# Score stacks moved by 64 bytes and score products widened to 64 rows, in an attention block gated by a bilinear GLU

## The chip, the cores and the metric

The kernel runs on one core of one Trainium2 chip. Its time is the device time of one execution in microseconds. Three runs of the kernel before the change gave 2594.28, 2596.97 and 2593.94 us; the median is 2594.28 us.

## What is computed

```
x: [1, 2048, 576]      D = 576, H = 32 heads of Dh = 18, F = 4608
xn   = layernorm(x)
q,k,v = heads of xn @ wqkv
s    = softmax(q k^T * Dh^-0.5) v   for each head;  s = concat(heads) @ wo
g    = silu(((xn @ w_gate) * (xn @ w_up)) @ w_down)
out  = x + s * g
```

Everything is float32. The kernel keeps float32 accuracy with TensorE's faster float32r format by splitting each operand into a high part (rounded to float32r) and a low part (the rest), and by summing the products high x high, low x high and high x low.

## The kernel before

**Prologue** (up to about 193 us). x is normalised, transposed with TensorE into columns, and split into high and low parts. `xc` (or `xcx`, for the first two chunks of 512 tokens) holds one chunk of columns: nine planes of 128 x 512. `qk_block` (L488) makes one 128-column block of q and k for one chunk with 14 whole-array matmuls (L493): weights from `wgu`, `wq1`, `wq2` or `ninth`, columns as the moving operand. Its high and low parts go to the DRAM tensor `sqk`. `v_block` (L550, matmuls at L556) makes v. There are nine column blocks and four chunks; blocks 4 and 5 take their weights from `wq2`, block 8 from `wq1`.

**Score stacks.** After the pool `early` is closed, three tiles of 128 partitions x 2048 float32 are made in the pool `stk`: `turning`, `whole0`, `whole1`. A stack holds, in partitions 0 to 53 and again in 64 to 117, three copies of 18 rows (one head's q or k, high or low). One matmul over these 54 rows (R = 54) gives the three split products at once. `load_stack` (L317) fills them from `sqk` with three DMAs each, issued on SP's queue. Before that, GpSimd sets all three tiles to 1.0 (L638, L641).

**Main stage** (about 193 to 2512 us). TensorE's array is used as two halves of 64 rows that run side by side, each with its own chain of matmuls. Four kinds of products are mixed in an order that a planner writes out by hand at build time, with fixed costs (0.231 us for a 512-column product, 0.132 us for a down product):

- `a_item` (L701, matmul L709): a 128 x 512 tile of scores, 54 rows, mostly on half 0. VectorE reduces it to a row maximum (L711). There are 2048 of them.
- `b_item` (L754, matmul L761): the same scores transposed, mostly on half 1, with 56 rows: rows 54 and 55 of the half carry the negative maximum (high and low part, written by `max_rows`, L733) against ones in the other operand. ScalarE takes the exponential (L763). There are 2048 of them.
- `gu_op` (L810, matmul L813): gate and up products of 64 rows x 128 by 64 x 512, 7776 of them; and `down_op` (L871, matmul L874): 64 rows x 128 by 64 x 288, 6912 of them.
- `pv_group` (L767, matmul L772): probabilities times v, on the whole array, in 7 us blocks.

Scores go to two banks `pa` and two banks `pb`, the rest to four banks `pg`; each product waits by semaphore until its bank has been emptied. **The end** (from 2512 us) multiplies by `wo` and writes out.

Where the operands lie, as byte offsets in a partition, and that offset modulo 256, from the program's memory map:

| tile | offset | mod 256 | role |
|---|---|---|---|
| xc | 59,552 and 77,984 | 160 | moving operand of L493 and L813; weights of L556 |
| wgu | 27,296 and 36,512 | 160 | weights of L493 and L813 |
| hs | 113,312 and 121,504 | 160 | weights of L874 |
| wd | 50,336 (half of its columns begin 1152 bytes further) | 160 and 32 | moving operand of L874 |
| wq1 | 185,760 | 160 | weights of L493 |
| wq2, xn | 220,128 and 209,888 | 224 | weights of L493; weights of the transposes |
| turning, whole0, whole1 | 204,768, 212,960, 221,152 | 224 | both operands of L709 and L761 |

Every slice of these tiles that a 512-column product takes begins a multiple of 256 bytes further on. `early` and `stk` are pools on the right side of the memory: they end at its upper end, one after the other in time.

Of the kernel before, what the change touches and what calls it, by code (L numbers as in the profile page):

```python
# [20 lines left out]
FT = mybir.dt.float32  # L21
# [20 lines left out]
def kernel(  # L42
# [10 lines left out]
    nc = tc.nc  # L53
# [46 lines left out]
    ep = early.enter_context(tc.tile_pool(name="early", bufs=1, side="right"))  # L100
# [18 lines left out]
    def w_split(raw, n, pool=None):  # L119

        if pool:
            w = pool.tile([128, n, 9, 128], FR, name=f"wq{n}")
        else:
            w = wpool.tile([128, 2, 9, 128], FR, name="wgu", bufs=2)
        ninth = pp.tile([128, 2, 128], FR, name="ninth", bufs=4)

        def piece(i, d, n, src, high=True, rest=True):
            if high:
                nc.scalar.activation(w[:, i, d:d + n, :], raw[:, i, src:src + n, :], AF.Copy)
            if not rest:  # L130
                return
            low = w[:, i, 4 + d:4 + d + n, :] if d < 8 else ninth[:, i:i + 1, :]
            op = nc.gpsimd.tensor_tensor(low, raw[:, i, src:src + n, :],
                                         w[:, i, d:d + n, :].bitcast(FT), op=OP.subtract)
            if behind:
                after(op, behind.pop(), "DVE's fast mode and Pool share a port")

        return (w, ninth), [(piece, a) for i in range(n) for a in ((i, 0, 4, 0), (i, 8, 1, 4))]
# [170 lines left out]
    R = 3 * DH  # L309
# [36 lines left out]
    def load_x(c, ts=range(4)):  # L346
        if ts[0] == 0:
            xin[c] = ep.tile([128, 4, D], FT, name="xin", bufs=2)
        for t in ts:
            nc.sync.dma_start(xin[c][:, t, :], x2[c * 512 + t * 128:c * 512 + t * 128 + 128, :])  # L350
# [28 lines left out]
    def norm(c, ts=range(4)):  # L379
        for t in ts:  # L380
            norm_stats(c, t)
        for t in ts:
            norm_apply(c, t)
# [3 lines left out]
    def to_columns(c):  # L387

        xn = xns.pop(c)
        if c < 2:  # L390
            xc = pp.tile([128, 9, 512], FR, name="xcx", bufs=2)
        else:
            xc = xcp.tile([128, 9, 512], FR, name="xc")
        xcs[c] = xc
        for k in range(5):
            if k < 4:
                p = bank("g", 3)
            else:
                p = bank("a" if nqk[0] % 2 else "b", 2)
                nqk[0] += 1  # L400
            for t in range(4):
                nc.tensor.transpose(p[:, t * 128:(t + 1) * 128],  # L402
                                    xn[:, t, k * 128:(k + 1) * 128], ident)
            if k < 4:
                nc.scalar.activation(xc[:, k, :], p, AF.Copy)
                nc.vector.tensor_tensor(xc[:, 4 + k, :], p, xc[:, k, :].bitcast(FT),
                                        op=OP.subtract)
            else:
                nc.scalar.activation(xc[:, 8, :], p, AF.Copy)
                nc.vector.tensor_tensor(xc[64:128, 8, :], p[64:128, :],  # L410
                                        xc[64:128, 8, :].bitcast(FT), op=OP.subtract)
# [76 lines left out]
    def qk_block(b, c):  # L488
        w, ninth = (t[:, b % 2] for t in wq[b // 2])
        p = bank("a" if nqk[0] % 2 else "b", 2)  # L490
        nqk[0] += 1
        for n, (a, e) in enumerate(QK_PAIRS):
            nc.tensor.matmul(p, w[:, a, :] if a < 9 else ninth, xcs[c][:, e, :], start=n == 0,  # L493
                             stop=n == len(QK_PAIRS) - 1)
        hl = pp.tile([128, 2, 512], FR, name="hl", bufs=3)
        nc.scalar.activation(hl[:, 0, :], p, AF.Copy)
        nc.vector.tensor_tensor(hl[:, 1, :], p, hl[:, 0, :].bitcast(FT), op=OP.subtract)
        g0 = blocks[b]
        for kind in range(2):
            lo, hi = max(g0, kind * D), min(g0 + 128, (kind + 1) * D)  # L500
            if lo < hi:
                dst = sqk[kind, :, lo - kind * D:hi - kind * D, c * 512:(c + 1) * 512]
                nc.sync.dma_start(dst.rearrange("h r s -> r h s"), hl[lo - g0:hi - g0].bitcast(FT))
# [40 lines left out]
    def v_split(h):  # L544
        cs = slice(h * HALF, (h + 1) * HALF)
        for k, d, lo in V_PARTS:
            nc.scalar.activation(vbox["w"][:, d, cs], vbox["raw"][:, k, :], AF.Copy)
        v_low(h)
# [18 lines left out]
    def w_now(i):  # L567
        wq[i], todo = w_split(raws[i], 1 if i == 4 else 2, ep if i == 2 else pp if i == 4 else None)
        for f, a in todo:
            f(*a)  # L570

    def w_fetch(i):
        raws[i] = w_load([(wqkv, b) for b in blocks[2 * i:2 * i + 2]])

    def x_store(c, ks):
        for k in ks:
            src = xcs[c][:, k, :].bitcast(FT)
            if k < 8:
                nc.sync.dma_start(sx[c, 2 * (k % 4):2 * (k % 4) + 2, :, k // 4, :].rearrange("b p s -> (b p) s"), src)
                if k % 4 == 0:  # L580
                    nc.sync.dma_start(sx[c, 9, :, k // 4, :], src[0:64])
            else:
                for part in range(2):
                    nc.sync.dma_start(sx[c, 8, :, part, :], src[64 * part:64 * part + 64])
# [22 lines left out]
    for c in range(NCH):  # L607
        if c + 2 < NCH:
            load_x(c + 2)
        for b in range(3):  # L610
            qk_block(b, c)
            if c == 0 and b == 0:
                w_now(2)
        if c + 1 < NCH:
            to_columns(c + 1)
        for b in range(3, 6):
            qk_block(b, c)
            if c == 1 and b == 3:
                v_split(c)
            if b < 5 and c + 2 < NCH:  # L620
                norm(c + 2, (0, 1) if b == 3 else (2, 3))
            if c in (1, 2):
                x_store(c, range(3 * (b - 3), 3 * (b - 2)))
            if c == 0 and b == 3:
                v_fetch(1)
            if c == NCH - 1 and b == 3:
                w_now(3)
        if c == 1:
            w_fetch(3)
            for t in range(4):  # L630
                v_block(t)
            w_fetch(4)
        if c == 2:
            w_now(4)
    early.close()
    stk = ctx.enter_context(tc.tile_pool(name="stk", bufs=1, side="right", reuse_waits="tile"))
    turning = stk.tile([128, S], FR, name="turning")
    nc.gpsimd.memset(turning.bitcast(FT), 1.0)  # L638
    whole = [stk.tile([128, S], FR, name=f"whole{i}") for i in range(2)]
    for w in whole:  # L640
        nc.gpsimd.memset(w.bitcast(FT), 1.0)  # L641
    vmore = ExitStack()
    more_rows(vmore.enter_context(tc.tile_pool(name="vmore", bufs=1, side="right")), 2)
    g_load(0)
# [46 lines left out]
    with ExitStack() as mid:  # L691
# [3 lines left out]
        def load_v(g):  # L695
            vt[g] = mp.tile([128, NT, 2 * (DH + 1)], FT, name="vt", bufs=2)
            nc.sync.dma_start(vt[g].rearrange("p t (h d) -> p t h d", h=2), sv[:, 2 * g:2 * g + 2, :].rearrange("(t p) h d -> p t h d", p=128))

        mx = {}

        def a_item(h, i, r=0, tag="a"):  # L701

            t, c = divmod(i, 4)
            if i == 0:
                mx[h] = mp.tile([128, NT, 4], FT, name="mx", bufs=1)
            q, k = stacks_of(h, r)
            p = bank(tag, 2)
            rows = slice(64 * r, 64 * r + R)
            nc.tensor.matmul(p, q[rows, t * 128:(t + 1) * 128], k[rows, c * 512:(c + 1) * 512],  # L709
                             start=True, stop=True)  # L710
            nc.vector.tensor_reduce(mx[h][:, t, c:c + 1], p, axis=AX.X, op=OP.max)  # L711
# [42 lines left out]
        def b_item(h, i, r=1, tag="b"):  # L754
            t, c = divmod(i, 4)
            if c % 2 == 0:
                pt[t, c // 2] = mp.tile([128, 2, 512], FT, name="pt", bufs=PT)
            q, k = stacks_of(h, r)
            p = bank(tag, 2)
            rows = slice(64 * r, 64 * r + R + 2)  # L760
            nc.tensor.matmul(p, k[rows, t * 128:(t + 1) * 128], q[rows, c * 512:(c + 1) * 512],  # L761
                             start=True, stop=True)
            nc.scalar.activation(pt[t, c // 2][:, c % 2, :], p, AF.Exp, scale=scale)  # L763
# [37 lines left out]

        hs, us = {}, {}
        TERMS = [t for b in range(9) for t in ((b, b, 0), (9 + b, b, 0), (b, b, 1))]
        half = [slice(0, 64), slice(64, 128)]

        def gu_start(r, n):
            ready(gdone, n)
# [607 lines left out]
    with ExitStack() as end:  # L1415
        ep = end.enter_context(tc.tile_pool(name="end", bufs=1, reuse_waits="tile"))
# [44 lines left out]
        for i, t in enumerate(order):  # L1461
# [4 lines left out]
            for h in range(2):  # L1466
                for n, (a, e) in enumerate(PAIRS):
                    w = wos[0][:, a, :] if a < 8 else wos[1][:, a - 8, :]
# [51 lines left out]
```

## Time and profile before

| | |
|---|---|
| median of three runs | 2594.28 us |
| profiled execution, span from first to last instruction | 2590.2 us |
| around the span (median less span) | 4.1 us |
| PE busy | 2582.3 us, 100% of the span |
| DVE, ACT, POOL busy | 1815.2, 1551.5, 677.0 us |
| TensorE clock granted | 1.000 |
| DMA moved | 435.65 MB, mean 168 GB/s |

The page gives for each engine its busy time, then the costliest groups of instructions by line, with their count, busy time and mean duration. The profiled execution's own time is its span and what lies around it. Matmuls overlap in the trace: a duration there runs from a matmul's start to its modelled end, longer than the distance to the next start, so rates are read from counts in a stretch of time or from distances between starts. L names a line of the kernel before. PEld is TensorE's weight load; a name such as `pa<-whole,turning` gives output and inputs.

### The profile page before, as it was taken

The page shows a single profiled execution, that of the slowest core. Times are in us where ns is not written, and L with a number is a line of the kernel's source. Part 1 is how long each engine was busy: PE and PEld are TensorE (multiplying, and loading weights), DVE is VectorE, ACT ScalarE, POOL GpSimd, SP SyncE. Part 2 cuts the span into 40 slices and gives each one's busy share as a digit, 9 for nine tenths or more (in the row PEclk, how much of TensorE's full clock was granted, in tenths as well). Part 3 has the DMA queues.
Part 4 walks back from the last instruction along what each step waited for, and adds up shares of the span by engine and source line. Part 5 has one row for each costly group of instructions (what it writes and reads, how often), then busy time and mean ns, then how long its engine had stood idle before and what let it go on. Part 6 is the DMA issues. An engine that isn't in the chain of part 4 may idle for free.

```text
span 2590.2 us, 59629 instructions
## 1 busy us (share of the span) xinstructions
PE 2582.3 (100%) x24439; PEld 2124.4 (82%) x24439; DVE 1815.2 (70%) x2996; ACT 1551.5 (60%) x3092; POOL 677.0 (26%) x701
## 2 busy tenths in 40 slices
PE   9999999999999999999999999999999999999999
PEld 8899877888888888888877877778888877877889
DVE  7209777776777778777777877777777777777238
ACT  4224677766766666666666666666666666666621
POOL 3114444434431222222111222111111222221016
PEclk9999999999999999999999999999999999999999
DMA  7899767677653444444454443444444444443357
GB/s 237 258 301 260 200 184 196 184 189 214 178 189 111 141 164 136 150 162 160 143 166 148 142 142 126 137 146 159 121 158 124 145 150 142 133 139 112 125 202 253
DMA packets 186641, 435.65 MB, mean 168 GB/s; under 512 B 51104, under 2 KB 112192, under 8 KB 156160
## 3 DMA queue, kind: packets, MB, share of 16 engines
q1 hardware_dynamic: 184208, 423.88, 53.0%
q0 software_dynamic: 2160, 7.96, 0.8%
q8 instruction: 192, 3.15, 0.5%
q14 instruction: 81, 0.66, 0.1%
HBM read 315.16 MB, written 111.35 MB: 165 GB/s over the span
## 4 chain that ended last, share of the span: by engine, by line
PE 98%; DMA 1%; DVE 1%; SPq 0%; ACT 0%; issue 0%; DVEq 0%
PE pg L813 36%; PE pg L772 17%; PE pg L874 16%; PE pa L709 11%; PE pb L761 9%; PE pb L493 2%; PE pa L493 2%; PE pg L556 2%; PE pg L1469 1%; PE pb L1469 1%; PE pa L1469 1%; DMA oin<-sot 0%; PE pa L761 0%; DMA xin<-in_A_x_dram 0%; PE pg L402 0%; DVE mx L711 0%
## 5 line engine op out<-in xcount | busy, mean ns | idle before, releaser
L711 DVE TENSOR_REDUCE mx<-pa 128x1 f32<-128x512 f32 x2016 | 1349.2, 687 | 330.5 <-PE pa L709 151.5
L813 PE MATMUL pg<-xc,wgu 64*128 64x512 f32 x7776 | 1441.6, 391 | 0.0
L763 ACT ACTIVATE pt<-pb 128x512 f32<-128x512 f32 x2005 | 1145.0, 602 | 469.0 <-PE pb L761 347.3
L813 PEld LDWEIGHTS pg<-xc,wgu 64*128 64x128 f32 x7776 | 1074.9, 186 | 51.9 <-issue 1.0
L874 PE MATMUL pg<-wd,hs 64*128 64x288 f32 x6816 | 879.0, 293 | 0.0
L874 PEld LDWEIGHTS pg<-wd,hs 64*128 64x128 f32 x6816 | 816.3, 185 | 11.3 <-issue 0.8
L709 PE MATMUL pa<-whole,turning 54*128 54x512 f32 x1999 | 783.2, 399 | 0.3 <-DVE mx L711 0.3
L761 PE MATMUL pb<-whole,turning 56*128 56x512 f32 x1978 | 775.2, 398 | 0.0
L772 PE MATMUL pg<-pt,vt 128*32 128x512 f32 x4096 | 453.3, 594 | 0.1
L709 PEld LDWEIGHTS pa<-whole,turning 54*128 54x128 f32 x1999 | 363.3, 184 | 76.6 <-issue 53.0
L854 POOL TENSOR_TENSOR hs<-us,hs 128x512 fp32r<-128x512 f32 x144 | 186.1, 1292 | 865.8 <-ACT hs L838 612.4
L901 POOL TENSOR_TENSOR acc<-acc,st 128x288 f32<-128x288 f32 x284 | 229.5, 810 | 606.3 <-ACT st L931 314.4
L761 PEld LDWEIGHTS pb<-whole,turning 56*128 56x128 f32 x1978 | 360.1, 185 | 5.8
L772 PEld LDWEIGHTS pg<-pt,vt 128*32 128x32 f32 x4096 | 126.2, 110 | 285.1 <-issue 279.2
L778 DVE TENSOR_TENSOR oc<-oc,pg 128x512 f32<-128x512 f32 x35 | 24.1, 688 | 221.1 <-PE pg L772 207.0
L257 POOL TENSOR_TENSOR wgu<-wraw,wgu 128x384 fp32r<-128x384 f32 x108 | 108.2, 1015 | 212.8 <-ACT wgu L256 118.1
L776 ACT ACTIVATE oc<-pg 128x512 f32<-128x512 f32 x32 | 19.2, 599 | 229.4 <-PE pg L772 222.0
L937 DVE TENSOR_TENSOR acc<-acc,pg 128x288 f32<-128x288 f32 x261 | 116.3, 448 | 38.2 <-PE pg L874 35.4
L830 DVE TENSOR_TENSOR us<-pg,us 128x512 f32<-128x512 f32 x144 | 98.7, 685 | 54.9 <-PE pg L813 52.2
L931 ACT ACTIVATE st<-pg 128x288 f32<-128x288 f32 x284 | 117.1, 413 | 27.2 <-PE pg L874 20.0
L823 ACT ACTIVATE us<-pg 128x512 f32<-128x512 f32 x143 | 85.5, 598 | 76.2 <-PE pg L813 63.8
L838 ACT ACTIVATE hs<-us 128x512 fp32r<-128x512 f32 x142 | 89.4, 630 | 16.2 <-DVE us L830 15.8
(164 smaller groups left out, 1294.5 us busy)
## 6 DMA issues: line engine op xcount, KB each, us to landing
wgu<-swg SPq DMA_DIRECT2D x102, 1152.0 KB
wd<-swd SPq DMA_DIRECT2D x50, 1152.0 KB
swg<-wgu SPq DMA_DIRECT2D x36, 1152.0 KB
whole<-sqk SPq DMA_DIRECT2D x192, 144.0 KB
turning<-sqk SPq DMA_DIRECT2D x384, 72.0 KB
swd<-wd SPq DMA_DIRECT2D x18, 1152.0 KB
sqk<-hl SPq DMA_DIRECT2D x32, 512.0 KB
xc<-sx SPq DMA_DIRECT2D x24, 512.0 KB
```

Source lines behind the costliest of these rows:

```text
L257: nc.gpsimd.tensor_tensor(w[:, 9 + b:12 + b, :], raw[:, b:b + 3, :], w[:, b:b + 3, :].bitcast(FT), op=OP.subtract)
L709: nc.tensor.matmul(p, q[rows, t * 128:(t + 1) * 128], k[rows, c * 512:(c + 1) * 512], start=True, stop=True)
L711: nc.vector.tensor_reduce(mx[h][:, t, c:c + 1], p, axis=AX.X, op=OP.max)
L761: nc.tensor.matmul(p, k[rows, t * 128:(t + 1) * 128], q[rows, c * 512:(c + 1) * 512], start=True, stop=True)
L763: nc.scalar.activation(pt[t, c // 2][:, c % 2, :], p, AF.Exp, scale=scale)
L772: nc.tensor.matmul(p[32 * c:32 * c + 32, :], vt[h // 2][:, t, 6 * (h % 2):6 * (h % 2) + 32], pt[t, c // 2][:, c % 2, :], start=t == ts[0], ...
L813: nc.tensor.matmul(ps, gw[n][half[r], a, :], xg[i][half[r], e, :], start=k == 0, stop=k == len(TERMS) - 1)
L854: nc.gpsimd.tensor_tensor(hj[:, 1, :], h32, hj[:, 0, :].bitcast(FT), op=OP.subtract)
L874: op = nc.tensor.matmul(ps[:, 0:HALF], hs[u][half[r], j, a, s * 128:(s + 1) * 128], dw[u][half[r], j, e, i * HALF:(i + 1) * HALF], start=( ...
L901: nc.gpsimd.tensor_tensor(a, a, st, op=OP.add)
L931: nc.scalar.activation(st, ps[:, 0:HALF], AF.Copy)
L937: nc.vector.tensor_tensor(a, a, ps[:, 0:HALF], op=OP.add)
```

## The change

Two empty tiles of 16 float32 (64 bytes) called `gap` are added, one at the end of `early`, one at the end of `stk`. Both pools grow by 64 bytes, so their tiles lie 64 bytes lower, at 160 modulo 256 (the stacks, `wq2`, `xn` and the rest of `early`). Both kinds of score products take all 64 rows of their half. So that the added rows give zero, the memsets now write only partitions 32 to 63 and 96 to 127, with 0.0 on one side of each product and 1.0 on the other: six memsets of 32 partitions in place of three of 128. The planner, its order and its costs are untouched.

```diff
@@ main part of the prologue
             if c == 0 and b == 0:
                 w_now(2)
+                ep.tile([128, 16], FT, name="gap")
...
     turning = stk.tile([128, S], FR, name="turning")
-    nc.gpsimd.memset(turning.bitcast(FT), 1.0)
     whole = [stk.tile([128, S], FR, name=f"whole{i}") for i in range(2)]
-    for w in whole:
-        nc.gpsimd.memset(w.bitcast(FT), 1.0)
+    stk.tile([128, 16], FT, name="gap")
+    for w, low, high in ((turning, 0.0, 1.0), (whole[0], 1.0, 0.0), (whole[1], 1.0, 0.0)):
+        nc.gpsimd.memset(w[32:64].bitcast(FT), low)
+        nc.gpsimd.memset(w[96:128].bitcast(FT), high)
...
+        half = [slice(0, 64), slice(64, 128)]
@@ a_item
-            rows = slice(64 * r, 64 * r + R)
+            rows = half[r]
@@ b_item
-            rows = slice(64 * r, 64 * r + R + 2)
+            rows = half[r]
```

More of the change, by code (lines that the diff above doesn't have):

```diff
@@ L803 @@
         TERMS = [t for b in range(9) for t in ((b, b, 0), (9 + b, b, 0), (b, b, 1))]
-        half = [slice(0, 64), slice(64, 128)]
         def gu_start(r, n):
```

## The prediction

> **What bounds the kernel now.** I read the page first: its engine rows, the chain that ended last, and the groups.
>
> ```profile
> span 2590.2 us, 59629 instructions
> ...
> PE 2582.3 (100%) x24439; PEld 2124.4 (82%) x24439; DVE 1815.2 (70%) x2996; ACT 1551.5 (60%) x3092; POOL 677.0 (26%) x701
> ...
> PE 98%; DMA 1%; DVE 1%; SPq 0%; ACT 0%; issue 0%; DVEq 0%
> ...
> L711 DVE TENSOR_REDUCE mx<-pa 128x1 f32<-128x512 f32 x2016 | 1349.2, 687 | 330.5 <-PE pa L709 151.5
> L813 PE MATMUL pg<-xc,wgu 64*128 64x512 f32 x7776 | 1441.6, 391 | 0.0
> ```
>
> PE is busy throughout and carries 98% of the chain; no other engine passes 70%. The order on PE is fixed, so the time is the sum of PE's steps, and whatever shortens a step shortens the span unless another engine then holds PE up. The duration in a group row (391 ns) is a pipelined one; what counts is the distance from one matmul's start to the next one's on the same half of the array. Two halves run side by side, so a stretch of T us holds n matmuls at a step of 2(T + 0.39)/n, the 0.39 us being those already under way at its start. The windows view gives n. Six stretches with gate/up and score products only, then three late ones with gate/up products only:
>
> ```profile
> 754.80:770.20 15.40, 15.40 (x136) 14.00 (x134) 13.72 (x22) 13.50 (x26) 5.74 (x5) 1.00 0.48 174
> 1182.60:1197.70 15.10, 15.10 (x134) 13.26 (x132) 13.41 (x21) 11.65 (x22) 3.88 (x5) 1.00 0.58 188
> 1249.40:1264.80 15.40, 15.40 (x136) 15.27 (x134) 13.86 (x22) 11.89 (x23) 1.67 (x2) 1.00 0.58 177
> 1674.50:1690.20 15.70, 15.70 (x138) 13.52 (x136) 14.65 (x22) 13.04 (x25) 2.10 (x2) 1.00 0.56 177
> 2102.20:2118.20 16.00, 16.00 (x140) 13.80 (x138) 15.14 (x25) 12.13 (x22) 2.10 (x2) 1.00 0.74 197
> 2239.90:2255.30 15.40, 15.40 (x136) 14.61 (x134) 14.50 (x23) 12.06 (x23) 1.75 (x2) 1.00 0.75 208
> 2452.60:2463.10 10.50, 10.50 (x96) 10.50 (x94) 1.10 (x2) 2.77 (x6) 1.28 (x1) 1.00 0.63 226
> 2481.10:2491.80 10.70, 10.70 (x98) 10.20 (x96) 2.31 (x5) 1.23 (x2) 1.83 (x2) 1.00 0.67 234
> 2499.80:2510.50 10.70, 10.70 (x98) 8.86 (x96) 1.15 (x2) 1.23 (x2) 1.28 (x1) 1.00 0.66 225
> ```
>
> The columns are the stretch, its length, then busy time and count of PE, PEld, DVE, ACT and POOL, the granted clock, the DMA share and GB/s. The clock is 1.00 in all nine, so it explains nothing. First six: 2(93.0 + 6 x 0.39)/820 = 232.5 ns. Last three: 2(31.9 + 3 x 0.39)/292 = 226.5 ns. The same array, the same number of columns, and 6.0 ns more per step wherever scores are mixed in.
>
> **Why 6 ns: the address.** PE's timeline in the prologue (start, length, line, operation, operands, shape and count, runs of one kind merged) shows the same two steps with whole-array products, where no scores exist:
>
> ```profile
> 101.08 3.11 PE L493 MATMUL pb<-xc,wgu 128*128 128x512 f32 x13
> ...
> 104.25 3.20 PE L493 MATMUL pa<-xc,wq 128*128 128x512 f32 x13
> ...
> 107.52 3.19 PE L493 MATMUL pb<-xc,wq 128*128 128x512 f32 x13
> ...
> 110.78 3.13 PE L493 MATMUL pa<-xc,wgu 128*128 128x512 f32 x13
> ...
> 113.97 3.11 PE L493 MATMUL pb<-xc,wgu 128*128 128x512 f32 x13
> ```
>
> Each block is 14 matmuls. Start to start: 3.17 us (226.4 ns each), then with the weights in wq2 3.27 and 3.26 (233.6 and 232.9), then 3.19 (227.9). In the memory map the moving operand xc lies 160 bytes above a multiple of 256, wgu too, wq2 224 above. So weights 64 bytes off the moving operand's place cost about 6.5 ns a matmul, and the first block afterwards is still 0.02 us long: the rhythm needs a few matmuls to come back. A change of bank, evictor and semaphore at each block's start costs nothing. The scores' stacks lie at 224, gate/up's operands at 160: each score loads weights from 224 under a stream from 160, and each next gate/up weight comes from 160 under a stream from 224. With one score in about 3.5 matmuls (19 of L709 among 134 in the stretch at 1182, and about as many of L761; rows further down) the rhythm is never regained; in the late stretches it is.
>
> The Trainium skill ("TensorE: Matmul & The Clock Gate", section "Step-by-step: what each phase is for") says the opposite: "Loading the next tile's weights doesn't steal SBUF read bandwidth from the running matmul." By that rule the place of the weights could not matter and this part would be worth nothing, 2594; the wq rows disagree, with 233.6 against 226.4 ns.
>
> **The change, part by part.**
>
> *The stacks 64 bytes lower, and 64 rows.* A score then has gate/up's shape (64 rows by 128, 64x512) and its place. I price it as a gate/up product. How many steps, and where the scores stand:
>
> ```profile
> 300.00:2390.00 2090.00, 1291.11 (x6779) 1.00 0.50 154
> 300.00:2390.00 2090.00, 751.17 (x1917) 1.00 0.50 154
> 300.00:2390.00 2090.00, 749.59 (x1911) 1.00 0.50 154
> ```
>
> The same view of L709 alone, in two pairs of neighbouring stretches:
>
> ```profile
> 1182.60:1197.70 15.10, 7.07 (x19) 1.00 0.58 188
> 1197.70:1206.00 8.30, 3.15 (x8) 1.00 0.89 273
> 1249.40:1264.80 15.40, 7.45 (x20) 1.00 0.58 177
> 1264.80:1275.00 10.20, 3.50 (x9) 1.00 0.82 201
> ```
>
> The first three rows are the windows view of L813, L709 and L761, one after the other, over the main stage: 10,607 products, 5,304 steps of each half. At 6.0 ns the ceiling is 31.8 us. The last four count L709 in the stretches with only gate/up beside the scores (39) and in those with down products too (17). So 70% of the scores stand where the 6.0 ns were measured: 22.3 us. For the 30% among down products the ends are 0 and 9.5 us; down products read half of wd's columns 1152 bytes further on, 128 off the others, and this stays, so the rhythm would be broken there anyway. I take a third, 3.2 us. The 106 us of the stage before 300 us add 106/2090 of 22.3, 1.1 us.
>
> *wq2 at 160.* The gap in the early pool moves wq2 as well. It serves 8 blocks of 14 (two column blocks, four chunks) at 3.27 instead of 3.18 us (3.17, and a little for the return): 0.7 us. Transposes of xn load from the same pool; their price is not shown by a changed neighbour, bounded by four chunks of 20 at wq2's 6.5 ns either way, 0.5 us; I take 0.
>
> *More rows by themselves.* The weight load, by the median of each line:
>
> ```profile
> L709 PEld LDWEIGHTS pa<-whole,turning x1999: 182/184/189, 193.5 to 2397.9; 54*128 54x128 f32 x200
> L813 PEld LDWEIGHTS pg<-xc,wgu x7776: 182/186/192, 193.6 to 2511.5; 64*128 64x128 f32 x200
> ```
>
> 2 ns more for 64 rows than for 54. Loads run under the matmul before; on the path it would be 2048 per half x 2 ns = 4 us. It is contained in pricing the score as a gate/up product, so 0 here.
>
> *Six memsets for three.* Each covers 32 partitions but the same 2048 elements; I take the duration of one of today's.
>
> ```profile
> 108.98 1.81 POOL L638 MEMSET turning<- 128x2048 f32 x1
> 110.83 3.56 POOL L641 MEMSET whole<- 128x2048 f32 x2
> 114.33 1.16 POOL L523 MEMSET vo<- 128x608 f32 x2
> 134.65 1.01 POOL L257 TENSOR_TENSOR wgu<-wraw,wgu 128x384 fp32r<-128x384 f32 x1 [19.15 <-ACT wgu L256]
> 122.32 1.09 SPq L322 DMA_DIRECT2D whole<-sqk  x3
> ```
>
> Three more are 5.4 us; POOL is idle for 19 us behind them. SP's first stack load would wait for the memsets, which end near 120.9 with those of vo, and issues at 122.32. If that cover of 1.4 us were gone, SP's queue (the sqk stores and later loads) would slip by the difference; but the first score comes at 193.5 (the L709 row above). Cost 0.
>
> *Sum.* 22.3 + 3.2 + 1.1 + 0.7 = 27.3 us of PE. What is late next is DVE, which reduces each score's bank: in the six mixed stretches it is busy 85.28 of 93.0 us, 92%, and in the 1674 and 2102 stretches 93 and 95%. With a step 2.5% shorter these two reach 96 and 97%, and a score there must more often wait for its bank. I let two stretches of six lose half: 0.83, and take 0.8. 27.3 x 0.8 = 21.8 us. The span goes from 2590.2 to about 2568.4; the runs shown have a median of 2594.28, 4.1 us above the span, which I carry over: 2572.5.
>
> **The rivals.**
>
> *A part only.* DVE takes back more than I allow, or the rhythm is broken by the down products in most places. DVE's 92% speaks for it; the 330.5 us that DVE is idle ahead of L711, 151.5 of them waiting for PE's L709, speak against. If only half of the pure stretches' 22.3 us comes, 11 + 0.7: 2582. Taken as 2582 to 2589.
>
> *No change.* The mixed stretches are slower because products of two kinds alternate (other banks, other evictors, more semaphores), not because of addresses. The late stretches differ from the mixed ones in that too, and in DVE's load. Then only wq2's 0.7 us is left: 2593.6. Against it stand the wq rows, where bank and evictor change at every block at no cost and only the place of the weights sets the step. The skill's sentence on weight loads gives this outcome as well.
>
> *Slower.* If place is nothing in half-array products, what is left is ten more rows in each score's weights: 2 ns on the path 4096 times, two side by side, 4 us, less 0.7: 2597.6. It decides once the address is worth less than 4 us. Against it: the load lies under the matmul before, and whole-array loads of 128 rows in the prologue run at the 226.4 ns step.
>
> **How the numbers follow.** The runs shown lie within 0.12%; 0.2% (5.2 us) is about what a measurement can tell. Forecast, 2562 to 2582: 0.68. More than that (the ceiling of 31.8 + 1.6 + 0.7 us unspoilt is 2560): 0.02. A part: 0.12. No change: 0.13. Slower: 0.05. So faster 0.82, same 0.13, slower 0.05. The range 2562 to 2589 holds 0.80; its ends are the ceiling nearly whole and the smallest part.
>
> **What would show it.** L709 and L761 read 64*128, 64x512. In stretches with only gate/up and scores the step, from counts as above, falls from 232.5 to 227 to 229 ns; the three late stretches keep 226.5. The wq blocks at 104 to 110 us start 3.17 to 3.18 us apart. L638's and L641's successors are six memsets of 32 partitions, 1.8 us each, and nobody waits for them. DVE's share in the mixed stretches rises to 94%. Wrong it would be if the mixed step stayed at 232.5 with stacks at 160 (then kinds, not places, set it), or if it fell and the span did not (then DVE or ACT holds PE, which would show as longer distances at scores).

## The result, and the profile after

The changed kernel takes 2576.34 us (median of 4 runs, 2575.75 to 2577.11) against 2594.11 us for the kernel before in the same session (4 runs): ratio 0.9932, 95% interval 0.9918 to 0.9946, 17.8 us faster. The forecast was 2572.5. The page of the changed kernel, in its span, engine rows, chain and costliest groups (L712 and L714 were L709 and L711, L764 was L761, L815 was L813):

```profile
span 2575.3 us, 59634 instructions
...
PE 2565.0 (100%) x24439; PEld 2096.9 (81%) x24439; DVE 1812.0 (70%) x2996; ACT 1548.8 (60%) x3092; POOL 682.1 (26%) x704
...
PE 98%; DMA 1%; DVE 1%; SPq 0%; ACT 0%; issue 0%; DVEq 0%
...
L714 DVE TENSOR_REDUCE mx<-pa 128x1 f32<-128x512 f32 x2016 | 1347.0, 687 | 319.5 <-PE pa L712 147.9
```

Nothing changed places: PE still carries 98% of the chain with the same 24,439 matmuls. The span is 14.9 us shorter; the other 3 us of the 17.8 lie in where each profiled execution stands in its own runs (3.9 us below the median before, 1.0 after), so the trace places 14.9 us. The windows view of the changed kernel, for the same six mixed stretches of the program and the same three of gate/up alone (columns as in the prediction):

```profile
750.50:765.70 15.20, 15.20 (x136) 14.34 (x135) 13.76 (x22) 13.53 (x26) 5.81 (x6) 1.00 0.49 182
1177.00:1191.90 14.90, 14.90 (x133) 13.20 (x132) 13.37 (x21) 11.63 (x22) 3.89 (x5) 1.00 0.58 190
1243.30:1258.40 15.10, 15.10 (x136) 14.84 (x134) 13.72 (x22) 11.94 (x23) 1.65 (x2) 1.00 0.58 178
1665.00:1680.50 15.50, 15.50 (x138) 13.04 (x136) 14.60 (x22) 13.00 (x25) 2.10 (x2) 1.00 0.57 172
2090.00:2105.80 15.80, 15.80 (x140) 12.66 (x138) 15.08 (x25) 12.13 (x22) 2.10 (x2) 1.00 0.73 198
2226.60:2241.80 15.20, 15.20 (x135) 14.32 (x134) 14.43 (x23) 12.03 (x23) 1.76 (x2) 1.00 0.79 212
2437.50:2448.00 10.50, 10.50 (x96) 10.50 (x95) 1.15 (x2) 3.08 (x6) 1.28 (x1) 1.00 0.62 225
2466.10:2476.80 10.70, 10.70 (x97) 10.70 (x96) 2.44 (x5) 1.23 (x2) 1.95 (x2) 1.00 0.65 234
2484.90:2495.60 10.70, 10.70 (x98) 8.86 (x96) 1.15 (x2) 1.23 (x2) 1.28 (x1) 1.00 0.69 232
```

The six: 2(91.7 + 6 x 0.39)/818 = 229.9 ns a step, where it was 232.5. The three: 2(31.9 + 3 x 0.39)/291 = 227.3, as before within a count. The mixed step came down by half of the 6 ns at most. One count more or less in each of six windows is 1.7 ns; so below the step is taken from the starts of all matmuls of a trace: twice the mean distance from one start to the next, whichever half they are on, over every stretch of more than 61 gate/up and score products with no other kind among them and at least 6 scores (50 of them, some 4900 steps). By that measure it went from 232.7 to 229.7. The share of short steps counts, in the same stretches, the distances to the next start on the same half that lie at 225 to 228 ns; which half a product runs on is read from the order of the program. It went from 17% to 55%: more than half of the steps take the short distance, called the short beat from here on, and the rest stay scattered.

Where the 14.9 us lie, by the same products in both traces: 9.7 us among gate/up and scores alone (6581 starts, 3290 steps of each half, 770 us of the span before), 4.7 us where scores stand among down products (1008 us), none in the PV blocks, the prologue or the end.

The prologue's blocks did what was said of them. PE's timeline of the changed kernel:

```profile
104.61 3.11 PE L493 MATMUL pa<-xc,wq 128*128 128x512 f32 x13
...
107.78 3.11 PE L493 MATMUL pb<-xc,wq 128*128 128x512 f32 x13
...
110.96 3.11 PE L493 MATMUL pa<-xc,wgu 128*128 128x512 f32 x13
```

3.17 and 3.18 us apart, where wq2 had 3.27 and 3.26. But the main stage starts no sooner. The rows of the changed kernel's L712 and L815, by line:

```profile
L712 PEld LDWEIGHTS pa<-whole,turning x1999: 182/184/188, 193.7 to 2383.5; 64*128 64x128 f32 x200
L815 PEld LDWEIGHTS pg<-xc,wgu x7776: 182/184/191, 193.8 to 2496.6; 64*128 64x128 f32 x200
```

The first score's load comes at 193.7 us, before it was 193.5. And 64 rows load in the 184 ns (median) that 54 took, while gate/up's loads, 64 rows before and after, fell from 186 to 184: the 2 ns that the prediction gave to ten more rows were not the rows'. The memsets, from POOL's timeline, and the first stack load, from SP's:

```profile
109.43 1.80 POOL L642 MEMSET turning<- 32x2048 f32 x1
...
118.68 1.81 POOL L643 MEMSET whole<- 32x2048 f32 x1
120.55 1.16 POOL L523 MEMSET vo<- 128x608 f32 x2
```

```profile
122.48 1.30 SPq L322 DMA_DIRECT2D whole<-sqk  x3
```

Six of 1.8 us, as costed; with those of vo they end at 121.7, and the first stack load issues at 122.48, before at 122.32. The cover held.

### The profile page after: what moved, and what is told of

Same layout as the page of the kernel before. It is cut to its first block, busy times and chain, and to the rows that moved or that the text cites. A ratio compares the mean times of both kernels' runs of the same rounds, so it can differ in the third digit from the quotient of the medians.

```text
span 2575.3 us, 59634 instructions
## 1 busy us (share of the span) xinstructions
PE 2565.0 (100%) x24439; PEld 2096.9 (81%) x24439; DVE 1812.0 (70%) x2996; ACT 1548.8 (60%) x3092; POOL 682.1 (26%) x704
## 4 chain that ended last, share of the span: by engine, by line
PE 98%; DMA 1%; DVE 1%; SPq 0%; ACT 0%; issue 0%; DVEq 0%
PE pg L815 35%; PE pg L775 17%; PE pg L876 16%; PE pa L712 11%; PE pb L764 8%; PE pb L493 2%; PE pa L493 2%; PE pg L556 2%; PE pg L1471 1%; PE pb L1471 1%; PE pa L1471 1%; DMA wgu<-swg 0%; DMA wos<-swo 0%; DVE mx L714 0%; DMA oin<-sot 0%; DMA xin<-in_A_x_dram 0%
## 5 line engine op out<-in xcount | busy, mean ns | idle before, releaser
L714 DVE TENSOR_REDUCE mx<-pa 128x1 f32<-128x512 f32 x2016 | 1347.0, 687 | 319.5 <-PE pa L712 147.9
L815 PE MATMUL pg<-xc,wgu 64*128 64x512 f32 x7776 | 1424.6, 389 | 2.0 <-DMA wgu<-swg 2.0
L815 PEld LDWEIGHTS pg<-xc,wgu 64*128 64x128 f32 x7776 | 1049.8, 184 | 57.4 <-issue 3.1
L876 PEld LDWEIGHTS pg<-wd,hs 64*128 64x128 f32 x6816 | 809.8, 184 | 11.9 <-issue 0.8
L712 PE MATMUL pa<-whole,turning 64*128 64x512 f32 x1999 | 777.6, 396 | 0.3 <-DVE mx L714 0.3
L764 PE MATMUL pb<-whole,turning 64*128 64x512 f32 x1978 | 769.0, 395 | 0.0
L712 PEld LDWEIGHTS pa<-whole,turning 64*128 64x128 f32 x1999 | 362.4, 184 | 82.5 <-issue 53.0
L903 POOL TENSOR_TENSOR acc<-acc,st 128x288 f32<-128x288 f32 x284 | 229.3, 810 | 601.4 <-ACT st L933 323.2
L764 PEld LDWEIGHTS pb<-whole,turning 64*128 64x128 f32 x1978 | 359.1, 184 | 6.0 <-ACT pt L766 0.2
```

Source lines behind the costliest of these rows:

```text
L815: nc.tensor.matmul(ps, gw[n][half[r], a, :], xg[i][half[r], e, :], start=k == 0, stop=k == len(TERMS) - 1)
L876: op = nc.tensor.matmul(ps[:, 0:HALF], hs[u][half[r], j, a, s * 128:(s + 1) * 128], dw[u][half[r], j, e, i * HALF:(i + 1) * HALF], start=( ...
L903: nc.gpsimd.tensor_tensor(a, a, st, op=OP.add)
```

## The experiments

The theory behind the forecast (P): a product's weights that lie elsewhere modulo 256 than the operand streaming at that time lose the short beat; rows are free. First rival (R): the count of rows does it, place is nothing. Later ones: both at once; and that VectorE holds the rest. Each kernel ran several times in one session with the kernel before, whose median was 2593.5 to 2594.1 us in these sessions; ratios and gains are within a session. All times in one table, with the mean mixed step and the share of steps at 225 to 228 ns, both from the starts as above:

| kernel | time, us | ratio to before, 95% | step, ns | short steps |
|---|---|---|---|---|
| before | 2594.1 | | 232.7 | 17% |
| changed | 2576.3 | 0.9932 (0.9918 to 0.9946) | 229.7 | 55% |
| place_only | 2593.2 | 0.9998 (0.9989 to 1.0007) | 233.1 | 11% |
| rows_only | 2589.7 | 0.9983 (0.9975 to 0.9992) | 232.6 | 16% |
| gap192 | 2586.0 | 0.9969 (0.9958 to 0.9981) | 232.7 | 14% |
| gap320 | 2575.7 | 0.9932 (0.9920 to 0.9945) | 230.0 | 54% |
| rows_a | 2587.7 | 0.9975 (0.9966 to 0.9984) | 231.8 | 31% |
| rows_b | 2590.4 | 0.9987 (0.9978 to 0.9996) | 232.4 | 29% |
| equal56 | 2578.8 | 0.9939 (0.9926 to 0.9953) | 229.7 | 57% |
| offset | 2575.1 | 0.9928 (0.9916 to 0.9941) | 229.3 | 58% |
| light_before | 2587.1 | 0.9975 (0.9966 to 0.9984) | 232.6 | 17% |
| light_after | 2563.2 | 0.9884 (0.9871 to 0.9898) | 227.8 | 84% |
| cut320 | 2578.5 | 0.9944 (0.9932 to 0.9957) | 229.6 | 57% |
| cut_offset | 2578.8 | 0.9945 (0.9932 to 0.9959) | 229.4 | 57% |

**place_only: the two gaps alone.** The kernel before with

```diff
+                ep.tile([128, 16], FT, name="gap")
...
+    stk.tile([128, 16], FT, name="gap")
```

> The stacks, wq2 and xn lie at 160 modulo 256 as in the changed kernel, but score products keep 54 and 56 rows and the memsets are those of before. Theory P (the place of the weights against the moving operand, modulo 256, sets the step): the whole gain is there, 2576 us, and the mixed stretches have a step of 229 to 230 ns as in the changed kernel. Theory R (products of 54 or 56 rows beside products of 64 rows break the rhythm): nothing but wq2's 0.7 us, 2593 us, mixed step 232 ns.

Nothing came: 0.9998. PE's timeline and the windows of the same six stretches, in this kernel:

```profile
104.02 3.11 PE L493 MATMUL pa<-xc,wq 128*128 128x512 f32 x13
...
107.20 3.11 PE L493 MATMUL pb<-xc,wq 128*128 128x512 f32 x13
...
110.37 3.11 PE L493 MATMUL pa<-xc,wgu 128*128 128x512 f32 x13
```

```profile
754.90:770.30 15.40, 15.40 (x136) 14.86 (x134) 13.70 (x22) 13.47 (x26) 5.71 (x5) 1.00 0.49 178
1183.00:1198.20 15.20, 15.20 (x134) 15.13 (x132) 13.45 (x21) 11.67 (x22) 3.90 (x5) 1.00 0.58 186
1249.90:1265.30 15.40, 15.40 (x136) 15.35 (x134) 13.88 (x22) 11.85 (x23) 1.69 (x2) 1.00 0.57 176
1675.00:1690.80 15.80, 15.80 (x140) 15.74 (x138) 14.74 (x24) 13.09 (x25) 2.10 (x2) 1.00 0.57 176
2103.30:2119.40 16.10, 16.10 (x140) 14.62 (x139) 15.22 (x25) 12.13 (x22) 2.09 (x2) 1.00 0.72 196
2241.00:2256.50 15.50, 15.50 (x137) 15.50 (x135) 14.57 (x23) 12.06 (x23) 1.76 (x2) 1.00 0.75 207
```

The place works in the prologue (3.18 and 3.17 us from block to block), where every product has 128 rows. In the mixed stretches the step is 2(93.4 + 2.34)/823 = 232.7 ns, unchanged. So place alone is not the cause, and P as it was put is refuted.

**rows_only: 64 rows alone.** The changed kernel without the two gaps.

```diff
-                ep.tile([128, 16], FT, name="gap")
...
-    stk.tile([128, 16], FT, name="gap")
```

> Score products take 64 rows with the new memsets, but nothing is moved: stacks, wq2 and xn lie at 224 modulo 256. Theory P: 2594 us, mixed step 232 to 233 ns. Theory R: 2577 us, mixed step 229 to 230 ns. If both parts are needed, both this run and the one with the place alone stand near 2594.

4 us and no change in the step: R falls too. The parts give 0.4 (within the measurement) and 4 us, together 17.8: neither is a cause by itself, each is a condition. The steps that begin at a score show it most plainly: 1% of them are short before and in place_only, 21% in rows_only, 49% in the changed kernel.

**gap192 and gap320: where the place must be.** The changed kernel with the second gap made larger, so that the stacks lie at 32, and again at 160 modulo 256.

```diff
-    stk.tile([128, 16], FT, name="gap")
+    stk.tile([128, 48], FT, name="gap")     # gap192
+    stk.tile([128, 80], FT, name="gap")     # gap320
```

> As the changed kernel, but the stacks lie 192 bytes lower instead of 64: at 32 modulo 256, 128 away from gate/up's operands. Theory P with the price of whole-array products at a distance of 128 (2 ns instead of 6.5): between the two kernels, about 2582 to 2588 us, mixed step 230.5 to 231.5 ns. If any place other than the old one will do: 2576 us. Theory R (rows alone): 2576 us.

> As the changed kernel, but the stacks lie 320 bytes lower instead of 64: another address, again 160 modulo 256. Theory P with a period of 256 bytes: 2576 us, the same as the changed kernel. If the distance counts modulo a larger power of two, or it is the neighbourhood of the memory's end that counts: another time, up to 2594 us.

At 128 off, 10 us of the gain go and the step is back at 232.7; the time is where P put it, the step is not. What is left lies, in the trace, where scores stand among down products (about 5 us there, nothing in the stretches of gate/up and scores). Half of wd's columns lie at 32 modulo 256 too, which may be why; no run tries that alone. At 256 further down all of the gain is there. So, with equal rows, place counts, and modulo 256. By the rule of the Trainium skill that the prediction weighed ("TensorE: Matmul & The Clock Gate", "Step-by-step: what each phase is for"), loads take no read bandwidth from the running matmul, and these two kernels should be alike; 2586.0 against 2575.7 disagrees.

**rows_a and rows_b: one kind of score at a time.** The changed kernel; in rows_a the exp products, in rows_b the max products get their old rows back.

```diff
-            rows = half[r]
+            rows = slice(64 * r, 64 * r + 56)     # b_item, rows_a
...
+            rows = slice(64 * r, 64 * r + 54)     # a_item, rows_b
```

> As the changed kernel, but the exp products of a head (b_item) take 56 rows again; the max products (a_item) keep 64, and all stacks stay 64 bytes lower. Theory A (on one half of the array, a mixed step keeps the short beat of about 227 ns only where the row counts of neighbouring matmuls are equal and the operands lie alike; each half by itself): the half whose scores have 64 rows keeps it, the other loses it; since a_item and b_item change halves from head to head, about half of the 17.8 us of the changed kernel is left: 2583 to 2588, mean mixed step 231 to 231.7 ns (232.7 before, 229.7 changed). Theory B (the two halves share one beat, and one half out of step spoils it for both): nothing is left beyond what the 64-row products brought by themselves: 2590 to 2593, mixed step 232.5 or more. Theory C (place alone does it and rows were only in the way by chance): 2575 to 2579.

> The counterpart: max products (a_item) take 54 rows again, exp products (b_item) keep 64, stacks 64 bytes lower. Theory A (each half by itself): about half of the gain, 2583 to 2588, mixed step 231 to 231.7 ns. Theory B (one shared beat): 2590 to 2593, mixed step 232.5 or more. Theory D (only the products that VectorE waits for matter, since its reduce of 128x512 is the mean bound of a mixed stretch at 93%): here no gain (2590 to 2594) and the full one in the kernel with 64-row max products.

D falls: with 64-row max products alone two thirds of the gain are missing. By time, rows_a lies in A's range and rows_b in B's. Taken half by half, the steps speak for A. In rows_a 52% of the steps are short on the half that has the 64-row scores and 9% on the other; in rows_b it is 46% and 13%, in the changed kernel 56% (max products) and 55% (exp products). So each half keeps or loses the beat for the most part by its own rows; the half with equal rows falls somewhat short of that in rows_b, and what disturbs it is open.

The two gains, 6.4 and 3.7 us, still do not add up to 17.8, and the traces show where much of the rest goes. A block of PV products takes the whole array, so the half that is done first must wait for the other. Taken from a half's last start and one short step (131.5 ns for a down product) to the block's first start, over 64 such blocks, the half with equal rows stands ready for 16.3 us in all in rows_a, where it is 8.8 in the changed kernel, and for 18.2 in rows_b, where it is 10.7. That is about 7.5 us gained on one half and waited out each time.

**equal56: equal, or full?** The changed kernel with 56 rows for the scores and for gate/up (the sums over the last 8 rows of each half are left out); down keeps 64.

```diff
+        few = [slice(0, 56), slice(64, 120)]
...
-            nc.tensor.matmul(ps, gw[n][half[r], a, :], xg[i][half[r], e, :], start=k == 0,
+            nc.tensor.matmul(ps, gw[n][few[r], a, :], xg[i][few[r], e, :], start=k == 0,
```

> As the changed kernel, but score products and gate/up products all take 56 rows of their half; the sums over the last 8 rows of each half are left out of gate/up and so of what follows. Theory A in the form that equal counts matter, whatever the count: as the changed kernel, 2574 to 2580, mixed step 229 to 230.5 ns. Theory A in the form that only a full half of 64 rows beats evenly: the gain goes, 2588 to 2596, and the stretches of gate/up alone (226.4 ns a step before) lengthen too, to 230 ns or more.

The groups of this kernel confirm the shapes:

```profile
L816 PE MATMUL pg<-xc,wgu 56*128 56x512 f32 x7776 | 1428.1, 389 | 2.0 <-DMA wgu<-swg 2.0
L712 PE MATMUL pa<-whole,turning 56*128 56x512 f32 x1999 | 779.2, 397 | 0.4 <-DVE mx L714 0.3
```

The gain is there with 56 rows: it is equality that counts, not fullness. It shows inside the kernel as well: among gate/up and scores (56 and 56) 9.5 us are gained, as in the changed kernel's 9.7; where scores stand among down products (56 and 64) 0.5 us, against 4.7.

**offset: set the halves apart.** Some mixed stretches of the changed kernel run wholly on the short beat (226.7 ns on the mean from 685.35 to 699.52 us), others not (233.8 from 1344.26 to 1357.47), and the slow ones often began with both halves within 20 ns of each other.

```diff
+            parts = ((0, 128), (128, 512)) if r and fresh[0] else ((0, 512),)
+            for lo, hi in parts:
+                nc.tensor.matmul(p[:, lo:hi], w, m[:, lo:hi], start=True, stop=True)
```

> As the changed kernel, but the first score product on the second half after each block of PV products is issued as two matmuls of 128 and 384 columns, which sets the second half's matmuls about 60 ns later against the first's; one matmul more for each of some 130 PV blocks (each some 15 to 30 ns more on that half by its load, 2 to 4 us in all if nothing hides it). Theory E (in the changed kernel stretches that begin with both halves together, 0 to 20 ns apart, stay at 232 to 234 ns, and those 30 to 70 ns apart fall to 227): mixed step 228 to 229, time 2568 to 2574. Rival F (the start of the halves only goes with the even beat and doesn't cause it): mixed step 229.5 to 230.5, time 2576 to 2582.

2575.1 and 229.3 ns: between the two, and not to be told from the changed kernel. The kernel has 66 matmuls more (24,505 for 24,439), so it set the halves apart at 66 blocks, not at the 130 expected. Inconclusive.

**light_after and light_before: VectorE's share.** Both kernels with the reduce over half the columns. The maximum is then over half of the keys, and the exponent is scaled by 0.25; PE's work is the same.

```diff
-            nc.vector.tensor_reduce(mx[h][:, t, c:c + 1], p, axis=AX.X, op=OP.max)
+            nc.vector.tensor_reduce(mx[h][:, t, c:c + 1], p[:, 0:256], axis=AX.X, op=OP.max)
```

> As the changed kernel, but VectorE's reduce takes the first 256 of the 512 columns of a max bank (the maximum is over half the keys, and the exponent is scaled by 0.25 so that nothing overflows; the scores, and PE's work, stay as they are). The reduce, 687 ns now, should take some 400 ns, so that no score product waits for VectorE. Theory W (what is left of the 6.0 ns in the changed kernel, 229.7 against 226.9 in gate/up alone, is the score products' wait for VectorE): mixed step 227 to 228, 2560 to 2568. Theory X (it is the beat of the two halves, and waits have nothing to do with it): mixed step 229 to 230, 2568 to 2577, less by what VectorE's own rows at stage ends give.

> The kernel before with the same lighter reduce (256 of 512 columns, exponent scaled by 0.25). Theory X: the step stays 232 to 233, and the distance to the changed kernel with the lighter reduce is again 15 to 20 us. Theory W with the prediction's 0.8 (VectorE takes a fifth of the gain back): the distance grows to 22 to 27 us. Rival (the odd steps before come from waits for VectorE, not from rows and place): step 227 to 229 here, distance under 5 us.

The group of the reduce and the six stretches, in light_after:

```profile
L714 DVE TENSOR_REDUCE mx<-pa 128x1 f32<-128x256 f32 x2016 | 838.0, 422 | 724.2 <-PE pa L712 476.9
```

```profile
746.40:761.60 15.20, 15.20 (x137) 15.12 (x135) 8.90 (x21) 13.51 (x26) 5.75 (x6) 1.00 0.49 180
1169.30:1184.10 14.80, 14.80 (x134) 13.03 (x132) 8.65 (x20) 11.72 (x22) 3.98 (x5) 1.00 0.58 191
1235.30:1250.30 15.00, 15.00 (x136) 14.04 (x134) 9.08 (x22) 11.81 (x23) 1.70 (x2) 1.00 0.57 179
1654.50:1669.80 15.30, 15.30 (x138) 14.85 (x136) 9.20 (x23) 13.00 (x25) 2.11 (x2) 1.00 0.57 178
2076.80:2092.10 15.30, 15.30 (x141) 15.29 (x139) 10.19 (x23) 11.98 (x22) 2.10 (x2) 1.00 0.73 206
2211.70:2226.90 15.20, 15.20 (x137) 15.13 (x135) 9.84 (x24) 12.07 (x23) 1.78 (x2) 1.00 0.76 211
```

DVE is busy 55.86 of 90.8 us, 62% where it was 93%, and the step is 2(90.8 + 2.34)/823 = 226.3 ns: that of gate/up alone (227.8 by the starts, over all 49 stretches of this kernel). So W holds in the changed kernel. In light_before the step stays at 232.6, so that there VectorE is not what makes the long steps. The distance between the two is 23.9 us, in W's range; with the whole reduce it is 17.8. Who waited for the reduce, as its line lists it, in us and times. Before:

```profile
  PEld pa L709: 6.4, 27
```

Changed:

```profile
  PEld pa L712: 6.8, 29
```

light_after:

```profile
  PEld pa L712: 0.5, 1
```

PE's waits for VectorE that the trace shows hardly grew, 6.4 to 6.8 us. Without them the kernel before gains 6.4 us (2593.5, its median in that session, to 2587.1), just these waits; the changed kernel gains 2576.3 - 2563.2 = 13 us, twice these waits. The other half fits the beat: after a wait the steps scatter for a while, and only in the changed kernel is there a beat to lose. The traces bear this out. In the changed kernel, of the next eight starts after a step of 245 ns or more, 19% are short steps, of the eight after them 33%, and of those more than 64 starts later 59%; in the kernel before it is 11, 21 and 16%. A rival is that VectorE's reading of the bank disturbs the steps directly. In light_after 83% of the steps are short where a reduce runs all through the step, and 83% where none does, which speaks against it; in the changed kernel it is 52% and 63%. No kernel was made to separate the two.

**cut320 and cut_offset: the down products' place.** The changed kernel with down's 576 columns cut 320 and 256; the second adds the edit of offset.

```diff
+    CUT = (0, 320, D)
...
-            op = nc.tensor.matmul(ps[:, 0:HALF], hs[u][half[r], j, a, s * 128:(s + 1) * 128],
-                             dw[u][half[r], j, e, i * HALF:(i + 1) * HALF],
+            op = nc.tensor.matmul(ps[:, 0:CUT[i + 1] - CUT[i]], hs[u][half[r], j, a, s * 128:(s + 1) * 128],
+                             dw[u][half[r], j, e, CUT[i]:CUT[i + 1]],
```

> As the changed kernel, but the down products' 576 columns are cut 320 and 256 instead of 288 and 288, so that both parts of a weight row start 160 above a multiple of 256 bytes (the second part of 288 starts 32 above one). If place counts for the down products as for the products before (131.5 against 133.5 ns for 288 columns), half of some 6900 products on two halves gain 2 ns each: 3 to 4 us faster, 2571 to 2574. Rival (stretches of down are set by something else, or the unequal parts break the beat as unequal rows did): 2575.5 to 2580.

> The changed kernel with both further edits: down products cut 320 and 256, and the first score on the second half after a PV block issued as 128 and 384 columns. The sum if both help and stand apart: 2570 to 2573. If neither does: 2575 to 2580.

2578.5 and 2578.8: no gain. Place for the down products is worth nothing that shows, or the unequal columns cost what it brings; the runs don't tell which. None of these kernels beats the changed one by more than the measurement can tell, light_after aside, which leaves out half of the maximum.

## Why the prediction came near, and where it was wrong

The time fell in the range and 3.8 us from the forecast, but the cause was told half wrong, and the sizes met by errors of opposite sign.

- *What bounds it* held: PE carries 98% before and after, and 14.9 us of the shorter span are distances between its starts.
- *"Why 6 ns: the address"* is the step that failed. The wq rows were read rightly, but all those products have 128 rows; the prologue could not show that unequal rows break the beat as well. place_only made the address alone and got 2593.2, the number of the rival "No change" (2593.6), whose reason, products of two kinds alternating, was nearer, though it named banks and evictors: the kinds differ in rows too, and equal56 shows that this is the trait.
- *"More rows by themselves"*, priced at 0 because the load's 2 ns are hidden: the load costs nothing more (184 ns either way), but the rows were the second condition, with 13 us of the 17.8 hanging on place once they are equal (rows_only to changed), and nearly all of it on rows once place is right (place_only to changed). That the change does both together saved the forecast; that was luck, since the reason given for it was place alone.
- *22.3 us in pure stretches* was mis-sized twice. The step gained 3.0 and not 6.0 ns. And the 70% of scores that were put there came from two pairs of stretches; counted over the whole order, 1690 of 4096 scores, 41%, stand where no down product is near, with 3290 steps for 3713. 3290 x 3.0 = 9.9 us, the trace's 9.7.
- *3.2 us among down products* was 4.7, and with the lighter reduce 11.9 (14.4 in light_after, 2.5 in light_before, each against before): above the end of 9.5 that I gave.
- *0.7 us of wq2*: the blocks came to 3.17 and 3.18 us as said, the main stage did not start sooner (193.7 against 193.5). Off the path: what the blocks gain is waited out before the first score.
- *The 0.8 for VectorE* was about right in size, 17.8/23.9 = 0.74. The place named was right too, with DVE's share in mixed stretches going from 92 to 93% (84.96 of 91.7 us). But the mechanism said more waits for banks, and the waits stayed at 6.4 and 6.8 us. They seem to cost the beat as well as themselves.
- *The 4.1 us around the span* were 1.0 after, which gave back 3 us of the sum's error. This too was luck: all four runs of the changed kernel are 1.7 to 1.8 us longer than their spans, and what goes beyond that is only how the profiled execution stood among its runs.

## What to carry to other kernels

When a short and a long step of the same instruction stand in one trace, list every trait in which the two places differ (address, rows, bank, neighbour) before pricing one; a comparison in which one trait is constant says nothing about it. Count where the instructions stand over the whole order, not in two samples. And when two conditions must hold together, try each alone: here they were worth 0.4 and 4 us apart and 17.8 together.

## What the runs showed of the hardware that was not expected

- Neighbouring 512-column products on one half of the array can keep starting 227 ns apart if they have equal row counts (56 and 56, or 64 and 64) and lie alike modulo 256 bytes: 54 to 57% of the steps of a mixed stretch then lie at 225 to 228 ns. If either differs (54 or 56 against 64 rows; 64 or 128 bytes off), 11 to 17% do, and the mean step is 232.6 to 233.1 ns.
- The beat can be lost and comes back slowly: with the same operands 55% of the steps are short beside a reduce of 687 ns, 84% beside one of 422 ns.
- Each half keeps the beat for the most part by itself: in rows_a 52% of the steps are short on one half and 9% on the other.
